# Attention feeding a SmeLU feed-forward on one core: four output tiles summed in two parts of d_ff, fillers joined, planner's times replaced

## The chip, the core and the metric

The kernel runs on one core of one Trainium2 chip. The metric is device time in microseconds (us), the median of three runs. A profile comes from one further execution, which has a time of its own; its span (first to last instruction) is a little shorter than that time. Engines are called as in the profile: PE (TensorE matmul), PEld (its weight loads), DVE (VectorE), ACT (ScalarE), POOL (GpSimd, which here only issues loads), SP (SyncE, which issues stores and some transposing DMAs).

## What is computed

```python
def sm_attn(qq, kk, vv):                      # softmax attention, scale 1/sqrt(64)
    ...
p_packed = sm_attn(p, k, v)                   # 32 packed rows per head attend to 576 tokens
out = sm_attn(q, p_packed, p_packed)          # 576 tokens attend to the 32 packed rows
x = out.transpose(0, 2, 1, 3).reshape(4608, 512)
h = x @ w_in                                  # (4608, 512) @ (512, 2048)
g = where(h >= 1, h, where(h <= -1, 0, (h + 1)**2 / 4))
return g @ w_out                              # (4608, 2048) @ (2048, 512)
```

q, k, v have 8 batches, 8 heads, 576 tokens and 64 channels; inputs and result are float32.

## The kernel before

**Stages of a batch.** For each of the 8 batches the kernel loads k, v and q (tokens folded 96 x 6), turns k and q (`trans`, on PE into PSUM and back by a copy to `kT`, `qT`; from batch 3 on by a transposing DMA that SP issues), forms the packed rows (`scores`: tile sp, exp by ACT into ex; `packed`: tile pk, then ppT and the reciprocal rs on DVE) and the weights of the second attention (`weights`: s, exp eT, column sums sm, ln, rc on ACT, then A on DVE, twice per batch). It never forms x: `mk` multiplies the packed rows by w_in (four tiles mp, cast to M), and `hidden_tile` (line 541) computes 128 rows of the hidden layer for the batch's 576 tokens as M times A. There are 16 hidden tiles per batch (index fi, along d_ff = 2048): four matmuls of 288 columns on PE (line 548), Prelu by ACT into x (line 553), an add-and-max on DVE or ACT (lines 558 and 560), and a min-and-multiply on DVE into hT (line 563).

**Output.** Two batches form a pair of 1152 tokens, nine output tiles of 128 tokens. `out_tile(pr, i)` (line 584) sums one of them: 16 steps, fi = 0 to 15, each one matmul of 128x512 (line 598, group "o"), hT as weights and the rows of w_out for that fi as moving data, into one PSUM buffer; then one copy of the sum to SBUF (`ob`, by ACT or DVE through the helper of line 319) and its stores from SP (line 604). Tiles 0 to 3 of a pair need the pair's first batch alone, tile 4 both. w_out comes in four loads of 512 rows, so fi 0 to 11 need the first three and fi 12 to 15 the last.

**Buffers.** PSUM has three buffers for everything else (`NW = 3`, pool psW) and two for output sums (`NO = 2`, pool psO). Prelu results have five (`NX`), `ob` six (`NB`).

**Order.** All instructions are handed out by `Plan`, when the kernel is built. Each piece of work is a task with an engine (or a choice of ACT and DVE, `both`), a cost in us from the table `C` (line 12), a key and its dependences. `run` (line 113) steps through an imagined time: of the tasks that are ready on an engine it takes the one with the lowest key that can start soon. Hidden tiles have the keys b to b + 1, output steps 100 and more, so an output step is taken where nothing else is ready. `land`, `load`, `half` and so on say when loads are thought to land, `slack` and `margin` how long after another engine's result PE is thought to be able to use it. Each engine then executes its list strictly in the order written; a wrong cost in the plan can put work that is ready behind work that isn't. The costs and times of the plan decide the order alone and no time on the chip.

**Fillers.** Until two output sums have been begun, where PE has nothing ready for more than a step, the plan writes matmuls of zeros of 256 columns (`idle`, line 661), each with its own weight load, which keep PE active.

**Loads.** POOL's queue issues, in this order: k, v, q of batch 0 in halves, w_in 0, w_in 1, w_out 0, w_in 2, w_out 1, w_in 3, w_out 2 (the third quarter), k of batch 1 in halves, v, q in halves, w_out 3 (the last quarter), the rest of p, and then k, q and v of later batches.

Of the kernel before, what the change touches and what calls it, by code (L numbers as in the profile page):

```python
# [8 lines left out]

C = dict(load=2.95, half=1.46, w_in=2.57, w_out=2.57, rest=1.25, out=9.0, p=4.05, land=1.75, xt=5.0, xland=11.0,
         tpp=0.06, tp=0.042, sc=0.034, pk=1.05, s2=0.25, sm=0.245, M=0.345, h=0.49, o=0.217, switch=0.05, join=0.15,
         pTc=0.1, Tca=1.12, Tcd=0.76, ex=0.82, ppT=0.42, ppo=0.41, ppa=0.4, ppd=0.2, rs=0.18, eT=0.74, ln=0.65, rc=0.68, A=0.82,
         Mca=1.0, Mcd=1.22, x=0.65, ta=0.683, td=0.457, hT=0.758, oba=0.585, obd=0.69,
         array=0.2, wake=1.2, warm=4.2, early=0.3, tell=0.04, feed=0.1, slack=0.6, margin=0.15, wait=0.5)
NW, NO, NX, NB = 3, 2, 5, 6
DW = 256
TURNED = 3


# [11 lines left out]
class Plan:  # L33
# [15 lines left out]
    def add(self, engines, cost, key, deps, fn, takes=None, readers=0, frees=None, mode=None, slack=None, after=0.0,  # L49
            holds=0.0):  # L50
        engines = (engines,) if isinstance(engines, str) else engines
        t = Task(engines, cost if isinstance(cost, dict) else {e: cost for e in engines}, key, deps, fn, takes, readers,
                 frees, mode, slack, after, holds)
        t.seq = len(self.tasks)
        self.tasks.append(t)
        return t

    def ready(self, t, e):
        at = 0.0
        for d in t.deps:  # L60
            if e == "PE":
                lag = 0.0 if d.on == "PE" else C["feed"] + (C["margin"] if t.slack is None else t.slack)
            else:
                lag = C["array"] if d.on == "PE" else C["tell"] if d.on != e else 0.0
            at = max(at, d.end + lag)
        if t.takes:
            rooms = self.rooms[t.takes]
            for j in range(len(t.readers)):
                room = rooms[(self.count[t.takes] + j) % len(rooms)]
                if room is None:  # L70
                    return None
                at = max(at, room + (C["feed"] if e == "PE" else 0.0))
        return at
# [39 lines left out]
    def run(self, idle):  # L113
        self.line = [t.seq for t in self.tasks if t.engines == ("DMA",)]
        left = {}
        given = {e: [] for e in self.ENGINES}
        for t in self.tasks:
            left[t] = len(t.deps)
            for d in t.deps:
                d.users.append(t)  # L120
            if not t.deps:
                for e in t.engines:
                    given[e].append(t)
        n = len(self.tasks)
        while n:
            best = None
            for e in self.ENGINES:
                c = self.choose(e, given, n)
                if c is not None and (best is None or c[0] < best[0]):
                    best = c[0], e, c[1]  # L130
            if self.count["O"] < 3:
                c, step = self.choose("PE", given, n), DW / 2400
                self.now["PE"] = max(self.now["PE"], C["wake"])
                if self.now["PE"] < C["warm"]:
                    step *= 2
                if (c is None or c[0] > self.now["PE"] + step + C["early"]) and best is not None and best[0] > self.now["PE"]:
                    idle()
                    self.now["PE"] += step
                    continue
            assert best is not None  # L140
            at, e, t = best
            t.on = e
            cost = t.cost[e]
            if e == "PE" and t.mode is not None and t.mode != self.mode:
                cost += C["switch"]
                self.mode = t.mode
            self.now[e] = at + cost
            t.end = at + cost + t.after + (C["land"] if e == "DMA" else 0.0)
            if e == "DMA":
                del self.line[0]  # L150
            self.log.append((at, at + cost, e, t))
            if t.takes:
                room = self.rooms[t.takes]
                t.slots = [(self.count[t.takes] + j) % len(room) for j in range(len(t.readers))]
                self.count[t.takes] += len(t.slots)
                for n_, j in zip(t.readers, t.slots):
                    room[j] = None if n_ else t.end + t.holds
            if t.frees is not None:
                f, j = t.frees
                f.gone[j] = max(f.gone[j], t.end)  # L160
                f.readers[j] -= 1
                if f.readers[j] == 0:
                    self.rooms[f.takes][f.slots[j]] = f.gone[j]
            if len(t.engines) > 1:
                t.fn(e)
            elif e in ("ACT", "DVE"):
                t.fn(e)
            else:
                t.fn()
            for x in t.engines:  # L170
                given[x].remove(t)
            for u in t.users:
                left[u] -= 1
                if left[u] == 0:
                    for x in u.engines:
                        given[x].append(u)
            n -= 1
# [3 lines left out]
def kernel(  # L181
# [10 lines left out]
    nc = tc.nc  # L192
    f32 = mybir.dt.float32
    bf16 = mybir.dt.bfloat16
    AF = mybir.ActivationFunctionType
    ALU = mybir.AluOpType
# [3 lines left out]
    d_model, d_ff = moe_w_in.shape  # L200
    n_tokens = out.shape[0]
    P = 128
# [13 lines left out]
    KF = d_ff // P  # L216
# [8 lines left out]
    att = ctx.enter_context(tc.tile_pool(name="att", bufs=2))  # L225
# [7 lines left out]
    plan = Plan({"W": NW, "O": NO, "x": NX, "ob": NB})  # L233
    PE, ACT, DVE, DMA, SP = "PE", "ACT", "DVE", "DMA", "SP"
    add = plan.add
# [10 lines left out]
    zeros = const.tile([P, FW], bf16)  # L246
# [3 lines left out]
    w_out_sb = const.tile([P, KF, d_model], bf16)  # L250
# [18 lines left out]
    hT = hid.tile([P, KF, 2 * S], bf16)  # L269
# [44 lines left out]
    def both(fns, cost_a, cost_d, key, deps, **kw):  # L314

        return add((DVE, ACT), {ACT: cost_a, DVE: cost_d}, key, deps, fns, **kw)

    def copy(out_, in_):
        return lambda eng: nc.vector.tensor_copy(out_, in_) if eng == DVE else nc.scalar.copy(out_, in_)  # L319
# [264 lines left out]
    def out_tile(pr, i):  # L584
        box, prev = {}, []
        bs = range(2 * pr + i * P // S, 2 * pr + ((i + 1) * P - 1) // S + 1)

        end = 2 * pr + 2 == B and i + 1 == NT
        w = d_model // 2

        def spare():
            box["o2"] = wide([P, w], f32, "o2")

        def step(fi):
            if fi == 0:
                box["o"] = psO.tile([P, d_model], f32, tag="o", name="o")
            for o, cs in [(box["o"][:, :w], slice(w)), (box["o2"], slice(w, d_model))] if end else [(box["o"], slice(d_model))]:
                nc.tensor.matmul(o, hT[:, fi, i * P:(i + 1) * P], w_out_sb[:, fi, cs], start=(fi == 0), stop=(fi == KF - 1))  # L598

        def done(eng):  # L600
            box["ob"] = ops.tile([P, d_model], f32, tag="ob", name="ob")
            copy(box["ob"], box["o"])(eng)
            for a, n, dst in out_rows(pr, i):
                nc.sync.dma_start(dst, box["ob"][a:a + n])

        def done_last(eng):

            for j, (eng, queue, o) in enumerate(((ACT, nc.scalar, box["o"][:, :w]), (DVE, nc.sync, box["o2"]))):
                ob = ops.tile([P, w], f32, tag="ob" + str(j), name="ob" + str(j), bufs=1)
                copy(ob, o)(eng)  # L610
                for a, n, dst in sorted(out_rows(pr, i), key=lambda x: -x[1]):
                    queue.dma_start(dst[:, j * w:(j + 1) * w], ob[a:a + n])
        if end:
            prev = [add(PE, 0.0, 100 + pr * NT + i, [K[B - 1, "h"][-1]], spare, takes="W", readers=1)]
        for fi in range(KF):
            t = add(PE, C["o"], 100 + pr * NT + i, [wrote[b, fi] for b in bs] + prev + [L["out", fi // 4]],
                    lambda fi=fi: step(fi), mode=0, takes="O" if fi == 0 else None, readers=1, slack=C["slack"])
            step_of[pr, i, fi] = t
            prev = [t]
            if fi == 0:  # L620
                owner = t
        both(done_last if end else done, C["oba"], C["obd"], b_key(pr, i), prev, frees=owner, takes="ob", holds=C["out"])

    def b_key(pr, i):
        return -0.5
# [32 lines left out]

    o = psO.tile([P, d_model], f32, tag="o", name="o")
    plan.count["O"] = 1  # L660
    plan.run(lambda: nc.tensor.matmul(o[:, :DW], zeros[:, :P], zeros[:, :DW], start=True, stop=True))  # L661


# [28 lines left out]
```

## Time and profile before

| What | Value |
|---|---|
| Three runs | 251.41, 252.23 and 252.58 us; median 252.23 us |
| The profiled execution | 250.97 us |
| Its span | 249.2 us |
| Outside the span (250.97 - 249.2) | 1.8 us |
| Granted TensorE clock | 1.0 of full speed in every slice |

Times inside the profile count from the span's start. Rows of the views by line give the engine, the operation, its output and inputs, the number of instructions, their busy time and the mean ns of one. A matmul's own duration contains the way through the array and overlaps the next one's, so what one matmul costs in a row of them is read from the length of the row. Idle time of an engine is listed by what ended it. A row of the timeline merges instructions of one kind that follow each other: start, length, what, how many, and in brackets the idle time before.

### The profile page before, as it was taken

What the parts mean: (1) busy time and instruction counts of PE and PEld (TensorE: products, weight loads), DVE (VectorE), ACT (ScalarE), POOL (GpSimd) and SP (SyncE); (2) the same over time, 40 slices, a digit from 0 to 9 for tenths busy, and PEclk for the clock granted to TensorE, in tenths of its full rate; (3) what the DMA queues carried; (4) which work ended last, traced back from release to release, by engine and by line L of the source; (5) the groups of instructions that cost most, each with busy time, mean ns of one, the idle gap of its engine ahead of it and who ended that gap; (6) DMA issues with size and microseconds to landing.
All of it is one profiled execution on the core that took longest, in us unless ns stands there. A gap on an engine that the chain in (4) does not pass through costs nothing.

```text
span 249.2 us, 5464 instructions
## 1 busy us (share of the span) xinstructions
PE 234.8 (94%) x2187; PEld 140.9 (57%) x2220; DVE 181.7 (73%) x308; ACT 182.5 (73%) x294; POOL 29.7 (12%) x44
## 2 busy tenths in 40 slices
PE   7887887999999999999999999999999999999993
PEld 5655465467546666556565656656556465544452
DVE  5456979788999899698979985998569878930000
ACT  3368888899888899798798984997859796841110
POOL 8632433012001301111101000000000000000000
PEclk9999999999999999999999999999999999999999
DMA  6999999999999999999999932312112112133223
GB/s 99 196 207 207 206 203 195 204 240 204 193 182 217 165 190 193 208 183 188 223 191 223 218 76 53 79 42 49 42 42 45 43 42 45 42 84 86 54 74 84
DMA packets 54825, 34.37 MB, mean 138 GB/s; under 512 B 27536, under 2 KB 50320, under 8 KB 54800
## 3 DMA queue, kind: packets, MB, share of 16 engines
q0 software_dynamic: 24672, 18.55, 49.9%
q1 hardware_dynamic: 29968, 15.34, 31.7%
q8 instruction: 17, 0.28, 0.4%
q10 hardware_dynamic: 160, 0.13, 0.2%
q14 instruction: 8, 0.07, 0.1%
HBM read 37.22 MB, written 9.44 MB: 187 GB/s over the span
## 4 chain that ended last, share of the span: by engine, by line
PE 76%; DMA 13%; ACT 3%; POOL 3%; issue 2%; DVE 2%; DVEq 0%; ACTq 0%; POOLq 0%
PE o L598 44%; PE h L548 22%; DMA w_in_sb<-in_moe_w_in_dram 7%; DMA q<-in_q_dram 6%; PE mp L493 3%; PE sp L397 2%; PE pk L417 1%; PE sm L461 1%; PE s L451 1%; PE tp L376 1%; DVE pT L319 1%; POOL w_in_sb L285 1%; ACT eT L456 1%; POOL k L259 1%; PE pk L423 1%
## 5 line engine op out<-in xcount | busy, mean ns | idle before, releaser
L598 PE MATMUL o<-w_out_sb,hT 128*128 128x512 bf16 (+1 forms) x559 | 135.6, 373 | 2.1 <-issue 1.1
L563 DVE SCALAR_TENSOR_TENSOR hT<-x 128x576 bf16<-128x576 f32 x128 | 93.2, 754 | 8.3 <-PE o L598 3.5
L598 PEld LDWEIGHTS <-hT 128*128 128x128 bf16 x592 | 56.1, 98 | 53.7 <-issue 4.8
L553 ACT ACTIVATE x<-h 128x576 f32<-128x576 f32 x128 | 77.2, 653 | 12.1 <-PE h L548 8.3
L548 PE MATMUL h<-A,M 128*128 128x288 bf16 x512 | 76.0, 286 | 1.4 <-ACT M L319 0.5
L548 PEld LDWEIGHTS <-M 128*128 128x128 bf16 x512 | 49.3, 98 | 24.1 <-ACT M L319 1.0
L558 DVE TENSOR_SCALAR x<-x 128x576 f32<-128x576 f32 x84 | 38.5, 459 | 11.8 <-ACT x L553 10.9
L319 ACT COPY ob<-o 128x512 f32<-128x512 f32 (+1 forms) x23 | 13.2, 576 | 32.1 <-PE o L598 32.1
L560 ACT ACTIVATE x<-x 128x576 f32<-128x576 f32 x44 | 29.4, 683 | 0.5
L319 DVE COPY ob<-o 128x512 f32<-128x512 f32 (+1 forms) x14 | 9.4, 669 | 25.8 <-PE o L598 25.7
L319 DVE CAST M<-mp 128x1024 bf16<-128x1024 f32 x16 | 19.4, 1218 | 2.8 <-PE mp L493 2.8
L319 ACT CAST M<-mp 128x1024 bf16<-128x1024 f32 x16 | 15.8, 1012 | 1.2 <-PE mp L493 1.2
L400 ACT ACTIVATE ex<-sp 96x768 bf16<-96x768 f32 x16 | 12.9, 806 | 3.2 <-PE sp L397 3.1
L472 DVE SCALAR_TENSOR_TENSOR A<-eT,rs,rc 128x576 bf16<-128x576 bf16 x16 | 13.0, 812 | 2.1 <-ACT rc L469 2.1
L259 POOL DMA_DIRECT2D k<-in_k_dram x10 | 7.5, 746 | 56.5 <-DMA kT<-k 40.0
L456 ACT ACTIVATE eT<-s,rs 128x576 bf16<-128x576 f32 x16 | 11.2, 736 | 2.8 <-PE s L451 2.6
L493 PE MATMUL mp<-w_in_sb,ppT 64*32 64x512 bf16 x256 | 10.7, 381 | 2.6 <-DMA w_in_sb<-in_moe_w_in_dram 2.2
L465 ACT ACTIVATE ln<-sm 128x576 f32<-128x576 f32 x16 | 10.4, 648 | 2.2 <-PE sm L461 2.1
L661 PE MATMUL o<-zeros 128*128 128x256 bf16 x68 | 10.6, 301 | 1.2 <-DVE zeros L247 1.2
L469 ACT ACTIVATE rc<-ln 128x576 f32<-128x576 f32 x16 | 10.9, 683 | 0.5
L259 POOL DMA_DIRECT2D q<-in_q_dram x10 | 7.6, 759 | 26.2 <-DMA qT<-q 12.7
L397 PEld LDWEIGHTS <-kT 128*128 128x128 bf16 x192 | 7.4, 98 | 2.6 <-DVE kT L319 0.6
(47 smaller groups left out, 114.4 us busy)
## 6 DMA issues: line engine op xcount, KB each, us to landing
out_dram<-ob SPq DMA_DIRECT2D x23, 192.0 KB, 2.5
v<-in_v_dram POOLq DMA_DIRECT2D x7, 576.0 KB, 18.4
k<-in_k_dram POOLq DMA_DIRECT2D x6, 576.0 KB, 12.4
q<-in_q_dram POOLq DMA_DIRECT2D x6, 576.0 KB, 14.0
out_dram<-ob SPq DMA_DIRECT2D x24, 128.0 KB, 2.8
w_in_sb<-in_moe_w_in_dram POOLq DMA_DIRECT2D x4, 512.0 KB, 14.7
w_out_sb<-in_moe_w_out_dram POOLq DMA_DIRECT2D x4, 512.0 KB, 16.8
out_dram<-ob SPq DMA_DIRECT2D x23, 64.0 KB, 2.0
```

Of the source, the lines that this page charges most:

```text
L259: nc.gpsimd.dma_start(tok[nm, b][:, hs].rearrange("p h c d -> p h (c d)"), SRC[nm][b, hs].rearrange("h (p c) d -> p h (c d)", c=NC))
L319: return lambda eng: nc.vector.tensor_copy(out_, in_) if eng == DVE else nc.scalar.copy(out_, in_)
L400: nc.scalar.activation(ex()[:, :, i].rearrange("p e x a n -> p e (x a n)"), box["sp"], AF.Exp, scale=scale)
L456: nc.scalar.activation(box["eT"], box["s2"][:, :, :HALF], AF.Exp, scale=rs()[:, g, 1:])
L472: nc.vector.scalar_tensor_tensor(A()[:, g], box["eT"], rs()[:, g, :1], box["rc"], ALU.mult, ALU.mult)
L493: nc.tensor.matmul(mp[a * NP:(a + 1) * NP, g], pp_of(y, h), w_in_sb[y * D:(y + 1) * D, h // 2, f * FW:(f + 1) * FW], start=True, stop=True)
L548: nc.tensor.matmul(h[:, hf, :HALF], T[b, "M"][:, g, fi * P:(fi + 1) * P], T[b, "A"][:, g, hf], start=(g == 0), stop=(g == G - 1))
L553: nc.scalar.activation(box["x"], box["h"][:, :, :HALF], AF.Prelu, bias=-1.0, alpha=0.5)
L558: nc.vector.tensor_scalar(x, x, 1.0, 0.0, ALU.add, ALU.max)
L560: nc.scalar.activation(x, x, AF.Relu, bias=1.0)
L563: nc.vector.scalar_tensor_tensor(hT[:, fi, col:col + S].rearrange("p (a t) -> p a t", a=2), box["x"], 1.0, box["x"], ALU.min, ALU.mult)
L598: nc.tensor.matmul(o, hT[:, fi, i * P:(i + 1) * P], w_out_sb[:, fi, cs], start=(fi == 0), stop=(fi == KF - 1))
```

## The change

Three things are done.

1. The output steps of tiles 0 to 3 of the first pair are cut at fi = 12. The first twelve steps are one PSUM sum; a new operation `kept` (by ACT or DVE) copies it to a new SBUF tile `part` (128x512 float32, four buffers) and so frees the PSUM buffer. The last four steps are a second sum in another PSUM buffer, and the final operation, on DVE alone, adds the PSUM sum and `part` into `ob`. All other output tiles are as before.
2. Fillers are gathered until the next real PE task and written as matmuls of up to 512 columns.
3. The plan's table `C` is replaced. Costs that differ: load 2.95 to 3.5666, land 1.75 to 2.0125, xt 5.0 to 6.5, pk 1.05 to 0.9765, s2 0.25 to 0.2862, M 0.345 to 0.2415, join 0.15 to 0.1604, td 0.457 to 0.489, obd 0.69 to 0.6276, tell 0.04 to 0.034, feed 0.1 to 0.085, slack 0.6 to 0.51, margin 0.15 to 0.1717.

```diff
+        cuts = [12, KF] if pr == 0 and i < 4 else [KF]
...
         def step(fi):
-            if fi == 0:
+            if fi == 0 or fi in cuts:
                 box["o"] = psO.tile([P, d_model], f32, tag="o", name="o")
...
-                nc.tensor.matmul(o, hT[:, fi, i * P:(i + 1) * P], w_out_sb[:, fi, cs], start=(fi == 0), stop=(fi == KF - 1))
+                nc.tensor.matmul(o, hT[:, fi, i * P:(i + 1) * P], w_out_sb[:, fi, cs], start=(fi == 0 or fi in cuts), stop=(fi + 1 in cuts))
+
+        def kept(eng):
+            box["part"] = att.tile([P, d_model], f32, tag="part", name="part", bufs=4)
+            copy(box["part"], box["o"])(eng)
 
         def done(eng):
             box["ob"] = ops.tile([P, d_model], f32, tag="ob", name="ob")
-            copy(box["ob"], box["o"])(eng)
+            if len(cuts) > 1:
+                nc.vector.tensor_tensor(box["ob"], box["o"], box["part"], ALU.add)
+            else:
+                copy(box["ob"], box["o"])(eng)
...
-                    lambda fi=fi: step(fi), mode=0, takes="O" if fi == 0 else None, readers=1, slack=C["slack"])
+                    lambda fi=fi: step(fi), mode=0, takes="O" if fi == 0 or fi in cuts else None, readers=1, slack=C["slack"])
...
-            if fi == 0:
+            if fi == 0 or fi in cuts:
                 owner = t
-        both(done_last if end else done, C["oba"], C["obd"], b_key(pr, i), prev, frees=owner, takes="ob", holds=C["out"])
+            if fi + 1 in cuts[:-1]:
+                first = both(kept, C["oba"], C["obd"], b_key(pr, i), prev, frees=owner)
+        if len(cuts) > 1:
+            add(DVE, C["obd"], b_key(pr, i), prev + [first], done, frees=owner, takes="ob", holds=C["out"])
+        else:
+            both(done_last if end else done, C["oba"], C["obd"], b_key(pr, i), prev, frees=owner, takes="ob", holds=C["out"])
...
-                    idle()
+                    fill += DW
                     self.now["PE"] += step
                     continue
...
+            while e == "PE" and fill:
+                w = min(fill, FILL)
+                idle(w)
+                fill -= w
...
-    plan.run(lambda: nc.tensor.matmul(o[:, :DW], zeros[:, :P], zeros[:, :DW], start=True, stop=True))
+    plan.run(lambda w: nc.tensor.matmul(o[:, :w], zeros[:, :P], zeros[:, :w], start=True, stop=True))
```

The first pair's nine tiles keep their 144 output matmuls, and all matmul shapes but the fillers' stay. Four copies (`kept`) are new, and four copies to `ob` become adds. The changed program's order, engine by engine, can be read from the built program; the prediction uses it.

More of the change, by code (lines that the diff above doesn't have):

```diff
@@ L8 @@
 from concourse._compat import with_exitstack
[L12 to L16, printed above, removed]
+C = dict(load=3.5666, half=1.46, w_in=2.57, w_out=2.57, rest=1.25, out=9, p=4.05, land=2.0125, xt=6.5, xland=11, tpp=0.06, tp=0.042, sc=0.034, pk=0.9765, s2=0.2862, sm=0.245, M=0.2415, h=0.49, o=0.217, switch=0.05, join=0.1604, pTc=0.1, Tca=1.12, Tcd=0.76, ex=0.82, ppT=0.42, ppo=0.41, ppa=0.4, ppd=0.2, rs=0.18, eT=0.74, ln=0.65, rc=0.68, A=0.82, Mca=1, Mcd=1.22, x=0.65, ta=0.683, td=0.489, hT=0.758, oba=0.585, obd=0.6276, array=0.2, wake=1.2, warm=4.2, early=0.3, tell=0.034, feed=0.085, slack=0.51, margin=0.1717, wait=0.5)
 NW, NO, NX, NB = 3, 2, 5, 6
-DW = 256
+DW, FILL = 256, 512
 TURNED = 3
@@ L123, in run @@
                     given[e].append(t)
-        n = len(self.tasks)
+        n, fill = len(self.tasks), 0
         while n:
```

## The prediction

> **What bounds the kernel now.** First the waits of PE, then the busy time by stretches.
>
> ```profile
> engine line waited for: us in total, times, longest us
> PE mp L493 <- DMA w_in_sb<-in_moe_w_in_dram: 2.2, 3, 1.0
> PE tp L376 <- DMA q<-in_q_dram: 1.6, 3, 0.6
> ...
> PE h L548 <- DVE pT L319: 0.3, 1, 0.3
> ```
> ```profile
> core 0: us, PE busy (x) PEld busy (x) DVE busy (x) ACT busy (x) POOL busy (x), PEclk, DMA share, GB/s
> 20.00:33.00 13.00, 11.26 (x85) 6.50 (x83) 10.93 (x19) 11.63 (x19) 3.94 (x6) 1.00 1.25 205
> 33.00:41.00 8.00, 6.86 (x122) 5.50 (x122) 6.42 (x13) 6.30 (x11) 2.68 (x4) 1.00 1.30 204
> 41.00:50.00 9.00, 7.87 (x100) 4.22 (x100) 7.42 (x9) 7.29 (x11) 1.53 (x2) 1.00 1.46 197
> 50.00:75.40 25.40, 24.63 (x276) 15.60 (x279) 22.99 (x39) 22.97 (x35) 2.32 (x3) 1.00 1.30 204
> 75.40:100.00 24.60, 24.39 (x231) 15.64 (x234) 23.26 (x39) 22.89 (x39) 3.43 (x4) 1.00 1.26 189
> 100.00:245.00 145.00, 143.39 (x1175) 82.11 (x1195) 100.19 (x166) 102.33 (x168) 3.92 (x5) 1.00 0.54 102
> ```
>
> PE waits for loads up to about 41 us and then hardly at all: 24.63 of 25.40, 143.39 of 145.00. So from 50 us the end is set by the PE work left over. Only early idle time can be won: 1.7 + 1.1 + 1.1 us in the three stretches to 50 us, and about 2 us more that is hidden because a lone matmul is booked as busy for its whole way through the array (0.38 us for an output step that costs 0.22 in a row). From 50 to 100 us DVE and ACT are nearly full too (90 to 95%).
>
> What one piece costs on PE is read where it runs in a row:
>
> ```profile
> 179.22 1.96 PE h L548 x16
> 181.18 3.88 PE o L598 x18
> ```
> ```profile
> 215.55 29.77 PE L598 MATMUL o<-w_out_sb,hT 128*128 128x512 bf16 x150
> ```
>
> Sixteen h matmuls take 1.96 us: a hidden tile (four) 0.49 us. Eighteen output steps take 3.88: 0.216 us each. The tail, 121 full and 32 half-width matmuls by the program's order (150 records), confirms it: 29.77 / 137 = 0.217.
>
> [...]
>
> **The change part by part.**
>
> ```profile
> 33.59 0.68 PE L376 MATMUL tp<-ident,k 96*128 96x96 bf16 x12 [0.51 <-DMA k<-in_k_dram]
> ...
> 37.53 1.24 PE L598 MATMUL o<-w_out_sb,hT 128*128 128x512 bf16 x5
> 38.61 0.86 PE L417 MATMUL pk<-ex,v 96*128 96x64 bf16 x24
> ...
> 40.86 0.68 PE L376 MATMUL tp<-ident,q 96*128 96x96 bf16 x12 [0.58 <-DMA q<-in_q_dram]
> ...
> 46.24 2.97 PE L598 MATMUL o<-w_out_sb,hT 128*128 128x512 bf16 x13
> 49.05 0.65 PE L548 MATMUL h<-A,M 128*128 128x288 bf16 x4
> ```
> ```profile
> 45.53 0.68 ACT L469 ACTIVATE rc<-ln 128x576 f32<-128x576 f32 x1
> ```
> ```profile
> 46.25 0.82 DVE L472 SCALAR_TENSOR_TENSOR A<-eT,rs,rc 128x576 bf16<-128x576 bf16 x1 [0.25 <-ACT rc L469]
> ```
>
> *More output steps early.* Before, two PSUM buffers hold tiles 0 and 1 up to fi 11, 24 steps, and no more can go until the last quarter of w_out lands. In the changed order 33 steps stand before pk (39 before the second tp of q) and 52 before batch 1's first hidden tile, where now 24 and 40 do. All other PE work up to that tile is the same, so 12 x 0.216 = 2.6 us less is left there.
>
> *When that tile starts.* Now at 49.05. PE first: up to the k turn at 33.59 the new order has 12 hidden matmuls more and one output step less (1.25 us), which fit in the idle time there, as M's third cast moves forward on ACT. From 33.59 to the end of tp q it has 16 output steps more and 12 h matmuls fewer: +2.0 us, against 0.6 us of idle time, so tp q comes about 1.2 us later (42.05). Then s, eT, sm, ln, rc and A follow with ACT's and DVE's durations, and rc ends near 47.6 instead of 46.2, A near 48.4 instead of 47.1. But now A waits 2 us for PE, which does 13 steps in front; in the new order only three stand there. First hidden tile at about **48.5 us**: 0.5 earlier. Lead 2.6 + 0.5 = **3.1 us**. I take 47.7 to 50 as its bounds (A straight behind today's end; 1.5 us of waits that I missed).
>
> *The copies.* Prices:
>
> ```profile
> L319 ACT COPY ob<-o 128x512 f32<-128x512 f32 x22 | 12.9, 585 | 29.3 <-PE o L598 29.3
> L319 DVE COPY ob<-o 128x512 f32<-128x512 f32 x13 | 8.9, 687 | 1.3 <-PE o L598 1.2
> L433 DVE TENSOR_TENSOR ppT<-pk,p 64x256 bf16<-64x256 f32 x7 | 2.8, 406 | 0.0
> L433 DVE TENSOR_TENSOR ppT<-pk,p 64x128 bf16<-64x128 f32 x2 | 0.6, 283 | 0.0
> ```
>
> Four `part` copies, three on DVE and one on ACT by the order: 3 x 0.687 + 0.585 = 2.6 us. The add at 128x512 isn't in the trace; its nearest kin read one PSUM and one SBUF operand, 283 and 406 ns for 128 and 256 elements, 0.96 ns an element: 406 + 256 x 0.96 = 0.65 us, about the copy that it replaces. Bounds 0.58 (ACT's copy) and 0.75 (the hT row below); I take 0.65, since the kin has the same operands. All four adds are on DVE; of the copies that they replace ACT does three now. Each add queues ahead of other DVE work: the first, behind tile 0's last four steps, stands ahead of both A of batch 1. Those steps need w_out's last quarter:
>
> ```profile
> 27.25 0.75 POOL L287 DMA_DIRECT2D w_out_sb<-in_moe_w_out_dram  x1 [1.28 <-DMA w_out_sb<-in_moe_w_out_dram]
> ```
> ```profile
> w_out_sb<-in_moe_w_out_dram POOLq DMA_DIRECT2D x4, 512.0 KB, 16.8
> ```
>
> It lands near 27.25 + 16.8 = 44. The steps are through at 45.8, the first rc of batch 1 not before 46.3, so the add hides; each us by which the load came later than 45 would delay A, M and PE by as much.
>
> *Fillers.* Joined pairs have the same columns; all stand before 20 us, where w_in's landing ends the waits (2.2 us above): 0, at most +-0.1.
>
> *Stores and loads.*
>
> ```profile
> 242.52 1.11 SPq L604 DMA_DIRECT2D out_dram<-ob  x2
> ```
>
> All eight stores of tiles 0 to 3 now stand ahead of batch 3's transposes on SP, at 0.55 us an issue, but the turned k isn't needed before batch 3's sp, after 70 us: 0. POOL's loads wait for turns and pk that come up to 1.2 us later while its queue has batch 2's loads still under way: 0, to 0.5 if a queue ran dry.
>
> *Batch 1's hidden stage, 48.5 to 75 us.* This takes part of the lead back.
>
> ```profile
> L563 DVE SCALAR_TENSOR_TENSOR hT<-x 128x576 bf16<-128x576 f32 x128 | 93.2, 754 | 8.3 <-PE o L598 3.5 <-ACT x L560 0.7 <-PE sp L397 0.5
> L553 ACT ACTIVATE x<-h 128x576 f32<-128x576 f32 x128 | 77.2, 653 | 12.1 <-PE h L548 8.3 <-DVE hT L563 3.4
> L558 DVE TENSOR_SCALAR x<-x 128x576 f32<-128x576 f32 x84 | 38.5, 459 | 11.8 <-ACT x L553 10.9
> L319 DVE CAST M<-mp 128x1024 bf16<-128x1024 f32 x16 | 19.4, 1218 | 2.8 <-PE mp L493 2.8
> L319 ACT CAST M<-mp 128x1024 bf16<-128x1024 f32 x16 | 15.8, 1012 | 1.2 <-PE mp L493 1.2
> ```
> ```profile
> 75.39 1.24 PE L548 MATMUL h<-A,M 128*128 128x288 bf16 x8
> ```
>
> Between batch 1's last A and batch 2's last A I summed both lists with start-to-start times (0.70 for hT, 0.56 for Prelu, 0.46 for the add-and-max; durations overlap by some 0.06 to 0.1 us): DVE 23.2 to 23.9 us, ACT 23.2 to 24.5, together 46.4 to 48.4. PE has fewer ready steps to bridge with: tiles 0 to 3 are nearly done, and tile 4 needs batch 1's hT. The order shows it: between the two sm and the 24 mp stand 3 steps, now 12 and sp. mp needs both ln to free PSUM, so PE idles there about 1 us. Walking ACT's queue (16 Prelu, two ex, four turns, then eT to rc, 24.5 us from 47.6) gives the last rc near 72.9 and A near 73.8, as now; then nine steps, and batch 2's first hidden tile at about 75.0, now 75.39. By then the order has 104 steps done against 95, less one sp of 12 (0.35 us): 9 x 0.216 - 0.35 = 1.6 us ahead, and 0.4 us earlier. Lead kept: **2.0 us**; 1.1 us is lost to waits.
>
> *Afterwards.* Batch 2's stage holds 25.6 us of PE work in the new order (61 output steps stand between its first and last part), DVE 22.6 and ACT 23.5. PE is the longer, as in all later stages. Lead stays 2.0 us, and the tail (tile halves, last stores) is as before.
>
> **Sum.** 250.97 - 2.0 = 249.0 us on the profiled execution's scale. That execution lies 1.26 us below the median of 252.23, so the forecast for a median is 252.23 - 2.0 = **250.2 us**.
>
> **Rivals.** One row more is needed, batch 3's first hidden tile:
>
> ```profile
> 95.92 2.34 PE L548 MATMUL h<-A,M 128*128 128x288 bf16 x16
> ```
>
> *The lead is kept whole.* If DVE and ACT hold 95% and the mp wait is filled, nothing is given back, and the present wait at 50.7 (h for pT, 0.3 to 0.5) goes too: 3.5 us, 248.7. For it: DVE and ACT reach 94% together from 75.4 to 100. Against: the few steps in front of mp.
>
> *DVE and ACT become the bound.* From batch 1's A (48.4) to batch 3's A they have, by the same sums, 47.9 + 46.5 = 94.4 us on two engines after the change, 85.5 before (two copies, three casts of M and three hidden tiles more inside the stretch). At a use u of both, A of batch 3 ends at 48.4 + 47.2/u. The new order has 6.8 us more PE work done at batch 3's first hidden tile, which now starts at 95.92. Lead = 6.8 + 95.9 - 48.4 - 47.2/u: 1.9 us at u = 0.90, 0 at 0.87, -1.2 at 0.85. So below 0.87 it is slower than before; at 0.84, with hidden tiles in the fixed order waiting for ACT's turns and casts, 252.23 + 1.9 = 254.1 us. For it: between the A of batches 1 and 2 these sums give 46.4 / (2 x 26.5) = 0.875 now. Against: PE was the one waited for there, and busy time gives 0.905 from 50 to 75.4 and 0.938 from 75.4 to 100.
>
> *Queueing eats it.* If batch 1's chain passes through the fuller PE, ACT and DVE queues 1.5 us later than I walked it (first hidden tile at 50), the lead at batch 2 is some 0.5 us: 251.7, no difference. That the cut does nothing, because the extra sums don't fit, is excluded by the order: 52 steps against 40.
>
> **How the numbers follow.** Forecast (gain 1.3 to 3 us) 0.48; lead whole 0.14; queueing, no difference 0.23; DVE and ACT the bound, slower 0.15. Within 0.5%, 1.26 us, a measurement of this kernel can't tell a change. Faster by over that 0.48 + 0.14 = 0.62, same 0.23, slower 0.15. The range takes in the whole lead with some 0.3 us of scatter (248.4) and u down to 0.87 (252.4); below and above lie about 0.2.
>
> **What would show it.** Right: 39 output steps before the second tp of q; batch 1's first hidden tile within 48 to 49.5 us; `part` copies and adds of 0.55 to 0.75 us; PE's waits around batch 2's sm and mp 1 us or more; DVE and ACT over 90% from 50 to 100 us; batch 2's first hidden tile near 75; no wait of PE after 100. Wrong: first hidden tile after 50, A of batch 1 queued behind the first add, waits of PE on hT or x between 75 and 100 us, or loads that land later than now.

## The result, and the profile after

Run in turns with the kernel before on one chip, the changed kernel took 250.05 us (median of 7 runs, 249.75 to 250.78), the kernel before 251.41 us (7 runs, 250.81 to 252.84). The ratio is 0.9933, its 95% interval 0.9906 to 0.9959: faster by 0.67%, about 1.7 us. The profiled execution took 249.87 us with a span of 247.8 us (before: 250.97 and 249.2).

The waits of PE in the changed kernel, then its busy time in the stretches that the prediction shows of before:

```profile
engine line waited for: us in total, times, longest us
PE mp L494 <- DMA w_in_sb<-in_moe_w_in_dram: 2.2, 3, 1.1
...
PE o L601 <- DVE hT L564: 0.6, 1, 0.6
PE h L549 <- ACT M L320: 0.5, 1, 0.5
```
```profile
core 0: us, PE busy (x) PEld busy (x) DVE busy (x) ACT busy (x) POOL busy (x), PEclk, DMA share, GB/s
20.00:33.00 13.00, 12.15 (x93) 7.36 (x92) 11.23 (x19) 11.75 (x19) 3.89 (x6) 1.00 1.26 206
33.00:41.00 8.00, 8.00 (x123) 5.58 (x122) 7.25 (x13) 6.49 (x10) 2.95 (x4) 1.00 1.31 206
41.00:50.00 9.00, 8.53 (x99) 4.00 (x97) 7.73 (x12) 6.63 (x10) 1.53 (x2) 1.00 1.46 195
50.00:75.40 25.40, 24.60 (x270) 14.95 (x269) 23.43 (x42) 23.87 (x36) 2.32 (x3) 1.00 1.28 209
75.40:100.00 24.60, 24.60 (x238) 14.59 (x237) 20.39 (x36) 22.41 (x36) 3.07 (x4) 1.00 1.27 209
100.00:245.00 145.00, 143.86 (x1199) 82.91 (x1197) 101.03 (x169) 106.63 (x173) 3.95 (x5) 1.00 0.54 98
```

The idle time of PE up to 50 us has shrunk from 1.74 + 1.14 + 1.13 = 4.0 us to 0.85 + 0 + 0.47 = 1.3 us: 2.7 us more work is done early. From 50 to 75.4 us PE is as busy as before (24.60, before 24.63), with 0.8 us of waits.

The timeline of PE in the changed kernel, from the second transposes of q to batch 3's first hidden tile:

```profile
42.25 0.68 PE L377 MATMUL tp<-ident,q 96*128 96x96 bf16 x12
...
49.06 0.65 PE L549 MATMUL h<-A,M 128*128 128x288 bf16 x4 [0.47 <-ACT M L320]
...
72.73 0.39 PE L601 MATMUL o<-w_out_sb,hT 128*128 128x512 bf16 x1 [0.56 <-DVE hT L564]
73.05 0.84 PE L494 MATMUL mp<-w_in_sb,ppT 64*32 64x512 bf16 x24
...
75.80 1.63 PE L549 MATMUL h<-A,M 128*128 128x288 bf16 x12
...
101.64 1.63 PE L549 MATMUL h<-A,M 128*128 128x288 bf16 x12
```

**The lead** tells where the time came from and where part of it went back. It is the PE work that stands before a batch's first hidden tile in one kernel and not in the other, less the time by which that tile starts later. Each piece is priced by what it costs in a row (0.216 us an output step and 0.123 an h, as in the prediction; a transpose tp 0.042, an sp 0.029).

- Batch 1: 12 steps, 2.6 us, and 49.06 against 49.05. Lead 2.6 us.
- Batch 2: 9 steps more and twelve sp (0.35 us) fewer, 1.6 us, and 75.80 against 75.39. Lead 1.2 us.
- Batch 3: 30 steps and 24 mp more and twelve sp fewer, 6.8 us, and 101.64 against 95.92, 5.7 later. Lead 1.1 us.
- The end: 249.2 - 247.8 = 1.4 us by the spans.

So 2.6 us are won before 49 us, 1.4 us are lost between 49 and 76 us, and nothing moves much after that.

### The profile page after: what moved, and what is told of

Read it like the earlier page. It is cut to its first block, busy times and chain, and to the rows that moved or that the text cites. A ratio compares the mean times of both kernels' runs of the same rounds, so it can differ in the third digit from the quotient of the medians.

```text
span 247.8 us, 5398 instructions
## 1 busy us (share of the span) xinstructions
PE 237.5 (96%) x2191; PEld 137.5 (55%) x2191; DVE 180.7 (73%) x312; ACT 186.2 (75%) x294; POOL 29.3 (12%) x44
## 4 chain that ended last, share of the span: by engine, by line
PE 79%; DMA 10%; DVE 6%; ACT 2%; issue 1%; POOL 1%; ACTq 0%; POOLq 0%
PE o L601 47%; PE h L549 21%; DMA w_in_sb<-in_moe_w_in_dram 8%; PE mp L494 3%; DVE hT L564 3%; DMA k<-in_k_dram 3%; PE pk L418 2%; PE sp L398 2%; PE tp L377 2%; PE sm L462 1%; DVE x L559 1%; PE s L452 1%; PE pk L424 1%; DVE pT L320 1%; ACT rc L470 1%
## 5 line engine op out<-in xcount | busy, mean ns | idle before, releaser
L601 PE MATMUL o<-w_out_sb,hT 128*128 128x512 bf16 (+1 forms) x592 | 144.5, 374 | 0.7 <-DVE hT L564 0.6
L564 DVE SCALAR_TENSOR_TENSOR hT<-x 128x576 bf16<-128x576 f32 x128 | 94.5, 755 | 5.4 <-ACT x L561 2.6
L549 PE MATMUL h<-A,M 128*128 128x288 bf16 x512 | 75.1, 286 | 0.5 <-ACT M L320 0.5
L559 DVE TENSOR_SCALAR x<-x 128x576 f32<-128x576 f32 x87 | 39.9, 458 | 11.0 <-ACT x L554 11.0
L561 ACT ACTIVATE x<-x 128x576 f32<-128x576 f32 x41 | 27.2, 683 | 0.1
L320 ACT COPY ob<-o 128x512 f32<-128x512 f32 (+1 forms) x19 | 10.9, 575 | 19.4 <-PE o L601 19.3
L320 ACT CAST M<-mp 128x1024 bf16<-128x1024 f32 x22 | 21.3, 1019 | 3.2 <-PE mp L494 3.2
L320 DVE CAST M<-mp 128x1024 bf16<-128x1024 f32 x10 | 12.1, 1220 | 6.4 <-PE mp L494 6.4
L260 POOL DMA_DIRECT2D q<-in_q_dram x10 | 7.4, 744 | 47.6 <-DMA qT<-q 33.3
L676 PE MATMUL o<-zeros 128*128 128x512 bf16 (+1 forms) x39 | 10.8, 406 | 1.2 <-DVE zeros L248 1.2
```

Of the source, the lines that this page charges most:

```text
L260: nc.gpsimd.dma_start(tok[nm, b][:, hs].rearrange("p h c d -> p h (c d)"), SRC[nm][b, hs].rearrange("h (p c) d -> p h (c d)", c=NC))
L549: nc.tensor.matmul(h[:, hf, :HALF], T[b, "M"][:, g, fi * P:(fi + 1) * P], T[b, "A"][:, g, hf], start=(g == 0), stop=(g == G - 1))
L559: nc.vector.tensor_scalar(x, x, 1.0, 0.0, ALU.add, ALU.max)
L561: nc.scalar.activation(x, x, AF.Relu, bias=1.0)
L564: nc.vector.scalar_tensor_tensor(hT[:, fi, col:col + S].rearrange("p (a t) -> p a t", a=2), box["x"], 1.0, box["x"], ALU.min, ALU.mult)
```

## The experiments

Two theories were set against each other. **The cut makes the gain**: the cut alone lets PE do more early, and the plan's new values matter little. **The gain needs both**: what counts is where the early steps stand, and the values of the plan decide that. Beside this stood the question of what takes 1.4 us back. In the table the steps are those before batch 1's first hidden tile, and the next column says when that tile starts; leads are in us against the kernel before (that at the end by the spans), and the ratio to the kernel before stands with its interval. No leads are given for the fillers alone, since no other piece of the order moves. Tiles and leads are of one execution each. Up to the first turn of batch 1's k the order of two tiles cut, of copies twice, of the add-and-max narrow and of turned by DMA is that of the changed kernel, yet that turn starts 0.44 us later in copies twice and 0.65 to 0.76 us later in the other three, behind later loads; their tiles and leads at batch 1 contain that.

| Kernel | Steps | Tile at | Lead batch 1 | Lead batch 2 | End | Ratio |
|---|---|---|---|---|---|---|
| before | 40 | 49.05 | | | | 1 |
| changed | 52 | 49.06 | 2.6 | 1.2 | 1.4 | 0.9933 (0.9906 to 0.9959) |
| cut alone | 52 | 52.90 | -0.3 | -2.6 | -2.6 | 1.0121 (1.008 to 1.0162) |
| times and fillers, no cut | 36 | 49.08 | -0.9 | -1.8 | -3.2 | 1.0121 (1.0084 to 1.0158) |
| fillers alone | 40 | | | | | 0.9987 (0.9958 to 1.0017) |
| two tiles cut | 55 | 49.83 | 2.5 | 0.9 | 0.7 | 0.9939 (0.991 to 0.9968) |
| old load and land | 64 | 55.58 | 0.2 | -2.3 | -2.4 | 1.0059 (1.0039 to 1.008) |
| old tell, feed, slack, margin | 52 | 49.77 | 2.4 | 0.1 | -0.2 | 0.9995 (0.9978 to 1.0012) |
| copies to part twice | 52 | 50.15 | 1.5 | -0.6 | -0.4 | 0.9992 (0.9973 to 1.0012) |
| copies to part narrow | 52 | 49.18 | 2.5 | 1.2 | 1.5 | 0.9927 (0.99 to 0.9954) |
| batch 1's add-and-max narrow | 52 | 49.73 | 1.9 | 1.1 | 1.3 | 0.9912 (0.989 to 0.9933) |
| turned by DMA from batch 2 on | 52 | 49.70 | 1.9 | -2.9 | -7.7 | 1.0252 (1.0216 to 1.0287) |

### The cut alone

Of the change only the cut: against the changed kernel, the old table `C` and fillers of 256 columns.

```diff
-DW, FILL = 256, 512
+DW, FILL = 256, 256
-C = dict(load=3.5666, ... margin=0.1717, wait=0.5)
+C = dict(load=2.95, ... margin=0.15, wait=0.5)
```

> The cut of the four tiles with the plan's old times and the old 256-column fillers. Theory (the cut makes the gain: more output steps go into PE's idle time before batch 1's first hidden tile, and part is given back while DVE and ACT work on batch 1): this order has 52 output steps before that tile, as the changed kernel, but 94 instead of 104 before batch 2's first, so some of the gain stays: a median about 250.6, 0.8 below the kernel before, first hidden tile of batch 1 at 49 to 50.5 us. Rival (the new times make the gain): no difference from the kernel before, about 251.4.

It took 254.45 us (before in the same turns 251.21), 1.2% slower than before, although 52 steps stand before batch 1's first hidden tile here too. PE's, ACT's and DVE's timelines of this kernel:

```profile
41.44 0.68 PE L381 MATMUL tp<-ident,q 96*128 96x96 bf16 x12
41.95 2.11 PE L605 MATMUL o<-w_out_sb,hT 128*128 128x512 bf16 x9
43.99 0.32 PE L456 MATMUL s<-qT,ppT 64*32 64x288 bf16 x8
...
49.18 0.68 PE L381 MATMUL tp<-ident,k 96*128 96x96 bf16 x12
...
50.35 0.67 PE L381 MATMUL tp<-ident,k 96*128 96x96 bf16 x12
...
52.90 0.65 PE L553 MATMUL h<-A,M 128*128 128x288 bf16 x4 [1.66 <-DVE kT L324]
```
```profile
43.30 0.40 ACT L324 COPY ppT<-ppT 64x256 bf16<-64x256 bf16 x1
```
```profile
52.09 1.42 DVE L324 COPY kT<-tp 128x1152 bf16<-128x1152 bf16 x2
```

Two things stand in the wrong place. The chain s, eT, sm, ln, rc, A, which everything waits for, starts 1.1 us later (s at 43.99, in the changed kernel at 42.85). Nine steps, 2.1 us, stand between the last transposes of q and the first s; but s needs the copy of ppT too, which in ACT's list stands behind other work and ends only at 43.70, so without the nine steps s could have come some 0.3 us earlier, not 2. And both transposes of batch 2's k stand before batch 1's first hidden tile; that tile needs one of the three PSUM buffers, and they are held (by these two and by tpp) until DVE copies kT out from 52.09 on, although batch 1's A has ended at 50.2. So the steps that were done early are paid for by a chain that starts late and a tile that waits for a buffer. The theory that the cut alone makes the gain fell here.

### The times and the fillers without the cut

```diff
-        cuts = [12, KF] if pr == 0 and i < 4 else [KF]
+        cuts = [KF]
```

> The new times and joined fillers without the cut. Theory (the cut makes the gain): 36 output steps stand before batch 1's first hidden tile, fewer than the 40 of the kernel before, so no gain: 251 to 252.3. Rival (the new times make the gain): as the changed kernel, about 250.0.

254.29 us, 1.2% slower than before. Batch 1's first hidden tile starts when it does in both other kernels (49.08), but only 36 steps stand ahead of it. PE of this kernel waits where the changed kernel has steps:

```profile
39.22 0.51 PE L418 MATMUL pk<-ex,v 96*128 96x64 bf16 x12 [0.68 <-ACT ex L401]
...
40.98 0.84 PE L494 MATMUL mp<-w_in_sb,ppT 64*32 64x512 bf16 x8 [0.45 <-DVE ppT L434]
...
44.50 0.40 PE L462 MATMUL sm<-eT,onesblk 128*128 128x288 bf16 x2 [0.59 <-ACT M L320]
```

With four steps fewer done, this kernel lies 0.9 us behind at batch 1. By batch 2 it is 1.8 us behind (PE waits 1.16 us for ACT's x at 51.41) and at the end 3.2; what takes the last 1.4 us was not traced.

The two halves are each a loss of 1.2%, which neither expectation of either run foresaw, and together a gain of 0.7%: they must not be added.

### Fillers alone

The kernel before with fillers gathered to 512 columns (the diff is against before).

```diff
-                    idle()
+                    fill += DW
```

> The kernel before with the fillers joined to 512 columns, nothing else. Theory (same columns, all before 21 us, where loads set the pace): no difference, 251.0 to 251.5. Rival (half as many weight loads free PE early): 250.7 or less.

251.41 us against 251.65: no difference. Of the three parts of the change this one does nothing that can be measured.

### Two tiles cut

```diff
-        cuts = [12, KF] if pr == 0 and i < 4 else [KF]
+        cuts = [12, KF] if pr == 0 and i < 2 else [KF]
```

> The changed kernel with tiles 0 and 1 alone cut: two copies fewer, the four adds become two; 55 output steps before batch 1's first hidden tile instead of 52, 104 before batch 2's first as before. Theory (the gain is steps placed early less what DVE and ACT give back): the same or up to 0.7 us faster than the changed kernel, 249.3 to 250.0. Rival (the gain goes with the number of tiles cut): half of it, about 250.7.

250.09 us, ratio 0.9939, no difference from the changed kernel that can be measured. With tiles 0 and 1 cut the plan puts 55 steps before batch 1's first hidden tile, three more than with four tiles cut. The gain of the change can be had with two copies and two adds; the number of cut tiles is not what sets it.

### More steps early

The changed kernel with the old `load` and `land`; the other new values stay.

```diff
-load=3.5666, land=2.0125
+load=2.95, land=1.75
```

> The changed kernel with the old load and land times, all other times new: the plan takes loads for earlier than they are and writes 64 output steps, not 52, ahead of batch 1's first hidden tile, most of them ahead of s of batch 1. Theory, amended after the first runs (early steps pay only where PE would idle; in front of batch 1's chain from q to A they delay it, and all that follows): s of batch 1 two or more us later than in the changed kernel, first hidden tile at 51.5 us or later, median 251.5 to 254. Rival (what counts is how many steps are done early): 12 more steps are 2.6 us, median about 247.5.

253.11 us, slower than before by 0.6%. There are 64 steps early, 24 more than before, but PE's timeline shows where:

```profile
43.40 1.46 PE L601 MATMUL o<-w_out_sb,hT 128*128 128x512 bf16 x6
45.34 0.51 PE L332 MATMUL tpp<-ident,p_nat 128*128 128x128 bf16 x6 [0.49 <-DMA p_nat<-in_p_dram]
...
46.24 1.69 PE L601 MATMUL o<-w_out_sb,hT 128*128 128x512 bf16 x7
47.86 0.32 PE L452 MATMUL s<-qT,ppT 64*32 64x288 bf16 x8
...
55.58 0.65 PE L549 MATMUL h<-A,M 128*128 128x288 bf16 x4 [0.57 <-DVE kT L320]
```

The second s comes at 47.86 (changed: 44.08), behind thirteen steps and behind the transposes tpp, which the plan with these values puts ahead of their load. Batch 1's first hidden tile starts 6.5 us later, behind three turns more and with a wait for DVE's kT, which eats the 6.7 us of more work (the steps and those turns). More early steps are not better: the same lesson as the cut alone, with the cut tiles, the fillers and most values as in the changed kernel.

### The old safety times

The changed kernel with the old values of the four times that say how long after another engine's result PE can use it.

```diff
-tell=0.034, feed=0.085, slack=0.51, margin=0.1717
+tell=0.04, feed=0.1, slack=0.6, margin=0.15
```

> The changed kernel, but of the plan's new values four go back: tell, feed, slack and margin, the times that say how long after another engine's result TensorE can use it. Its order has 52 output steps before batch 1's first hidden tile as the changed kernel has, and 93 before batch 2's (104 in the changed kernel). Theory (what decides is how many steps stand where TensorE would idle without standing ahead of batch 1's chain; the load and cost values give that, and these four only shift a few steps): batch 1's first hidden tile at 48.8 to 49.8 us, ratio to the kernel before 0.990 to 0.997. Rival (the four values are what places batch 1's and batch 2's chains right; without them output steps or turns stand ahead of the chain again, as with the old plan): batch 1's or batch 2's first hidden tile over 1 us later than in the changed kernel, ratio 1.002 to 1.012.

251.27 us against 251.31, so all of the gain is gone; the ratio lies between the two expectations. The first theory's number for batch 1 holds (49.77 us, lead 2.4), but its ratio doesn't, and the rival's delay of over 1 us is not there. Here the gain is lost in batch 1's stage. PE of this kernel:

```profile
72.26 0.61 PE L601 MATMUL o<-w_out_sb,hT 128*128 128x512 bf16 x2 [0.88 <-DVE hT L564]
...
74.02 0.39 PE L601 MATMUL o<-w_out_sb,hT 128*128 128x512 bf16 x1 [0.39 <-DVE hT L564]
74.48 0.67 PE L549 MATMUL h<-A,M 128*128 128x288 bf16 x4
```

Batch 2's first hidden tile starts 1.3 us earlier than in the changed kernel, but with 11 steps fewer in front of it (93, changed 104), and PE waits 0.88 and 0.39 us on hT. The lead there is 0.1. Values that differ by 0.1 us or less decide over the whole gain.

### The copies to part made twice

```diff
             copy(box["part"], box["o"])(eng)
+            copy(box["part"], box["o"])(eng)
```

> The changed kernel with each copy to part done twice: six DVE copies and two on ACT instead of three and one, 2.6 us more work on the two engines, the same order on PE. Theory (DVE and ACT take part of the lead back in batch 1's stretch): batch 1's second A and its first hidden tile come 0.5 to 1.5 us later, and the median is 0.4 to 1.2 us above the changed kernel's, 250.5 to 251.3. Rival (the copies lie beside other work and cost nothing): 250.0, first hidden tile at 49.1 as in the changed kernel.

251.26 us, the gain is gone (ratio 0.9992); 2.6 us more of copies cost 1.5 us by the ratios (0.9992 against 0.9933) and 1.8 by the spans (249.6 against 247.8). PE of this kernel, with the instruction order of the changed kernel:

```profile
38.24 0.81 PE L601 MATMUL o<-w_out_sb,hT 128*128 128x512 bf16 x3 [0.51 <-DVE part L320]
...
50.15 0.65 PE L549 MATMUL h<-A,M 128*128 128x288 bf16 x4 [0.47 <-ACT M L320]
...
53.87 0.33 PE L377 MATMUL tp<-ident,k 96*128 96x96 bf16 x4 [0.77 <-DVE pT L320]
```

The first hidden tile comes 1.1 us later than in the changed kernel. Of this 0.44 is not the copies': the turn of k is that late (34.20, changed 33.76), before any copy to `part` and behind a longer wait for w_in (1.25 us at 30.16, changed 0.60 at 29.70). Then PE waits 0.51 us for a PSUM buffer that the doubled copy holds. 0.7 us more are lost between this tile and batch 2's, beginning with the wait for pT, whose copies stand behind a doubled one on DVE. Without the late load the spans give 1.4 us, close to the 1.5 of the ratios.

### The copies to part made narrow

Each copy to `part` takes 64 of 512 columns, and the adds are plain copies. This leaves the first twelve steps out of the result of tiles 0 to 3.

```diff
-            copy(box["part"], box["o"])(eng)
+            copy(box["part"][:, :64], box["o"][:, :64])(eng)
-                nc.vector.tensor_tensor(box["ob"], box["o"], box["part"], ALU.add)
+                nc.vector.tensor_copy(box["ob"], box["o"])
```

> The changed kernel, same order, but part takes 64 of 512 columns and the adds are copies of the second sum alone; left out is the first twelve steps' contribution to tiles 0 to 3. Theory (the four copies on DVE and ACT cost about 0.6 us of time for each us, as doubling them showed): 0.8 to 1.3 us faster than the changed kernel, 248.8 to 249.3. Rival (the first copy lies in idle time and only the second was dear): 250.0.

249.86 us, ratio 0.9927: no gain over the changed kernel that can be measured, and batch 2's first hidden tile at 75.81 (changed 75.80). The copies as they are cost nothing that can be measured; made twice they cost. So they lie in slack, and what slack is left behind them doesn't hold a second set.

### Batch 1's add-and-max made narrow

The changed kernel's order, but DVE's add-and-max of batch 1 takes 64 of 576 columns (the rest of that operation is left out for batch 1).

```diff
-                nc.vector.tensor_scalar(x, x, 1.0, 0.0, ALU.add, ALU.max)
+                xs = x[:, :, :32] if b == 1 else x
+                nc.vector.tensor_scalar(xs, xs, 1.0, 0.0, ALU.add, ALU.max)
```

> The changed kernel with the same order, but VectorE's add-and-max on batch 1's hidden tiles works on 64 of 576 columns (leaves out the rest of that step for batch 1, so half of that batch's activation is not computed). This frees VectorE of about 0.35 us per tile, some 4 us in all, between 52 and 75 us. Theory (the part of the lead that is lost before batch 2 is lost on VectorE, which from 61 to 72.7 us works back to back and on which the output step at 72.73 waits): batch 2's first hidden tile starts 0.7 to 1.4 us earlier than in the changed kernel (near 74.4 to 75.1 instead of 75.80), and the time is 0.7 to 1.4 us below the changed kernel's, ratio to the kernel before about 0.988 to 0.9905. Rival (ScalarE's list of Prelus, casts, turns and then eT, ln, rc sets batch 2's first hidden tile, VectorE only happens to be full): that tile starts within 0.3 us of 75.80, and the ratio stays at 0.992 to 0.995.

249.43 us, ratio 0.9912, between the two expectations. The groups by line and PE's timeline of this kernel:

```profile
L560 DVE TENSOR_SCALAR x<-x 128x64 f32<-128x64 f32 x12 | 2.3, 189 | 0.9 <-ACT x L554 0.8
```
```profile
69.56 0.59 PE L602 MATMUL o<-w_out_sb,hT 128*128 128x512 bf16 x2 [0.16 <-DVE hT L565]
...
71.47 0.41 PE L462 MATMUL sm<-eT,onesblk 128*128 128x288 bf16 x2 [0.21 <-ACT eT L457]
...
73.41 0.41 PE L494 MATMUL mp<-w_in_sb,ppT 64*32 64x512 bf16 x8 [0.33 <-ACT ln L466]
...
75.91 1.63 PE L549 MATMUL h<-A,M 128*128 128x288 bf16 x12
```

Twelve operations of 0.46 us became 0.19, 3.2 us of DVE. In this execution loads landed late (k is turned at 34.43, changed 33.76) and batch 1's first hidden tile stands at 49.73, so the stage itself is compared: from there to batch 2's it takes 26.18 us, in the changed kernel 75.80 - 49.06 = 26.74. That is 0.56 us back of the 1.4 lost. Batch 1's last hT ends 1.45 us earlier by the same measure, and the wait of 0.56 for hT has gone, but in its place PE waits for ACT's eT and ln, 0.21 and 0.33. The ratios give 0.5 us too, though their intervals overlap. So DVE holds this stage by some 0.5 us, and right behind it ACT does.

### Turned by DMA from batch 2 on

Batch 2's k and q are turned by SP's transposing DMA, as from batch 3 on, which takes 48 transposes off PE and their copies off DVE and ACT.

```diff
-TURNED = 3
+TURNED = 2
```

> The changed kernel with batch 2's k and q turned by the transposing DMA as batch 3's are: 48 transposes leave PE (2.0 us) and four copies leave ACT (4.2 us), all in the stretch of batch 1's hidden tiles. Theory (DVE and ACT take the lead back there): 2 to 3.5 us faster than the changed kernel, 246.5 to 248.0. Rival (the transfers between 48 and 70 us are full, turned k and q land too late and batch 2's first hidden tile moves back): 250 or more, with waits of PE on turned k or q.

258.1 us, 2.5% slower. PE of this kernel:

```profile
77.56 4.92 PE L601 MATMUL o<-w_out_sb,hT 128*128 128x512 bf16 x22
82.41 0.44 PE L452 MATMUL s<-qT,ppT 64*32 64x288 bf16 x16
...
86.54 0.64 PE L549 MATMUL h<-A,M 128*128 128x288 bf16 x2 [1.70 <-DVE A L473]
```
```profile
88.00:90.00 2.00, 2.00 (x9) 1.21 (x9) 0.68 (x2) 1.08 (x2) 0.00 (x0) 0.50 1.23 176
```

With this the plan places batch 2's attention late: s at 82.41 (changed: 68.07), behind 22 steps in a row, and batch 2's first hidden tile at 86.54. It therefore says nothing on whether the turns' copies take the lead back. Order in another place explains only part of the loss: the lead is -2.9 us at batch 2's first hidden tile, but -7.7 at the end. Behind that tile PE's granted clock, the third number from the end in the row by stretch, is 0.50 from 88 to 92 us (0.59 in the two before, 0.80 from 92 to 95), which alone costs some 3 us, as an estimate from PE's busy time in these stretches. The six runs have mean clocks of 0.986 to 0.991. The rest was not traced.

## Why the prediction was right, and where it was not

**The twelve steps, 2.6 us: right.** 52 steps stand there, PE's idle time to 50 us fell by 2.7 us, and the second tp of q came at 42.25 (forecast 42.05).

**"First hidden tile at about 48.5 us: 0.5 earlier": wrong.** It starts at 49.06, as before. ACT's and DVE's timelines of the changed kernel:

```profile
44.46 0.74 ACT L457 ACTIVATE eT<-s,rs 128x576 bf16<-128x576 f32 x1 [0.47 <-PE s L452]
...
47.42 0.68 ACT L470 ACTIVATE rc<-ln 128x576 f32<-128x576 f32 x1
48.01 1.91 ACT L320 CAST M<-mp 128x1024 bf16<-128x1024 f32 x2
```
```profile
48.14 0.82 DVE L473 SCALAR_TENSOR_TENSOR A<-eT,rs,rc 128x576 bf16<-128x576 bf16 x1 [0.52 <-ACT rc L470]
48.88 0.68 DVE L320 COPY part<-o 128x512 f32<-128x512 f32 x1
```

The second eT waits 0.47 us for s, which stands behind two mp and two steps; rc ends at 48.1 (forecast 47.6) and A at 48.96 (48.4). Then the first cast of M, which ACT makes only after rc, ends about as late as A (48.01 and 1.0 us), and PE waits 0.47 us for it. The chain of batch 1 was walked without the steps inside it and without the cast behind it. The bounds, 47.7 to 50, held it.

**Batch 1's stage, "1.1 us is lost to waits": right in kind, 1.4 us in size.** DVE is busy for 92% and ACT for 94% of 50 to 75.4 us, as forecast. The wait sits on hT (0.56, at 72.73) and not on ln at mp; taking DVE's load away brings 0.56 us back. Both errors add: the lead at batch 2 is 1.2 us where 2.0 was forecast (tile at 75.80 instead of 75.0).

**"Lead stays 2.0 us": it does stay** (1.2, 1.1, then 1.4 at the end). From 75.4 to 100 us PE is the one that is full (24.60 of 24.60), DVE only 83%, so "over 90% to 100 us" was too high, and the rival in which DVE and ACT become the bound stayed out. That PE would not wait after 100 us came true: its last matmul ends at 243.86, and from 100 us to there it is busy all the time, where before 1.6 of 145 us were idle; this is where the lead goes from 1.1 to 1.4 us.

**The copies and adds at 0.65 us each, hidden: right.** The groups by line:

```profile
L610 DVE TENSOR_TENSOR ob<-o,part 128x512 f32<-128x512 f32 x4 | 2.8, 688 | 0.3 <-PE o L601 0.2
L320 DVE COPY part<-o 128x512 f32<-128x512 f32 x3 | 2.1, 689 | 0.2 <-PE o L601 0.2
```

The add, with one operand in PSUM and one in SBUF, measures 0.688 us, inside its bounds of 0.58 to 0.75; the copy to `part` of the same size takes 0.689 us on DVE. The narrow copies showed that they cost nothing as they are, the doubled ones that no second set would be hidden.

**Fillers at 0: right,** by their own experiment.

**The time.** 250.2 us was forecast and 250.05 measured. Part of that closeness is luck: the forecast took 2.0 us from a median of 252.23, the turns beside the changed kernel gave 251.41 for before, and the gain was 1.4 us by the medians and 1.7 by the ratio. Some tenths of a us of this may be no lead at all but the clock, which the working left out (see the last section). What the working had right is that it counted the steps in the finished order. Had it argued from the cut alone, as "12 more steps early, 2.6 us", it would have forecast the same for the cut alone, which is 3.2 us slower than before.

**Which values of the table matter** was narrowed, not settled. Without `load` and `land` the kernel is 0.6% slower than before, without the four safety times it equals before; the six costs (`pk`, `s2`, `M`, `join`, `td`, `obd`) and `xt` weren't tried by themselves, and of the 1.4 us in batch 1's stage only 0.56 are put to an engine by a run; the other 0.8 are not.

## What to carry to other kernels

Where a bound engine idles early, moving independent work there paid in these runs only where it stood behind, not ahead of, the chain that the next stage starts with: count the pieces between the chain's links in the finished order of each engine that the chain passes, since the same 52 early steps gained 0.7% in one order and lost 1.2% in another. When an enabling change and a table of scheduling costs are changed together, measure each alone before crediting either. And follow a lead from stage to stage: of the 2.6 us won here by batch 1's first hidden tile 1.4 were given back in the next stretch, in which DVE is busy for 92% and ACT for 94%.

## What the runs showed of the hardware

**PE fell to half its clock after an idle time of 1.95 us.** In the profiled execution of the cut alone a load of q came late. PE's timeline and its granted clock by stretches (the third number from the end of a row):

```profile
15.18 1.14 PE L381 MATMUL tp<-ident,q 96*128 96x96 bf16 x12 [1.95 <-DMA q<-in_q_dram]
```
```profile
15.00:15.50 0.50, 0.32 (x5) 0.32 (x6) 0.00 (x0) 0.00 (x0) 0.08 (x1) 0.62 1.23 201
15.50:18.00 2.50, 2.50 (x35) 2.19 (x33) 1.26 (x4) 0.85 (x2) 1.07 (x2) 0.50 1.24 206
18.00:18.50 0.50, 0.50 (x3) 0.14 (x1) 0.50 (x2) 0.00 (x0) 0.20 (x1) 0.50 1.25 207
18.50:19.00 0.50, 0.50 (x17) 0.14 (x16) 0.36 (x1) 0.06 (x1) 0.00 (x0) 0.97 1.24 207
```

Twelve transposes took 1.14 us instead of 0.68. The half clock lasts 0.38 + 2.5 + 0.5 + 0.03 = 3.4 us by these rows. Later in the same execution a wait of 1.66 us (at 52.90) left the clock at 1.00. With batch 2 turned by DMA it fell as well, behind 83.07 to 86.54 us, where PE is busy for 0.8 of 3.5 us, and stayed low for 6.8 us by the same working. Why the clock fell at these places and not at the wait of 1.66 us, no run shows. In the cut alone only 0.46 us of the delay was left by the next transposes of k (34.05 us, before 33.59), and its runs with a mean clock of 1.0 took 253.65 and 255.8 us, so the clock isn't what made that kernel slow.

**The kernel before loses clock more often than the changed order.** A stretch of 3.4 us at half clock lowers the mean clock of 249 us by 0.007, to 0.993. Beside the experiments, on three chips, the kernel before ran 62 times: 39 runs with a mean clock of 0.996 or more, median 251.2 us, and 23 with 0.993 or less, median 252.3. The changed order (the changed kernel, the copies made twice or narrow, the add-and-max narrow) ran 32 times, never below 0.996. So part of the measured gain may come from this, some 0.4 us as an estimate (23 of 62 times 1.1 us). No trace shows where the kernel before loses its clock or why the changed order keeps it, so this stays open.

**The same four copies cost nothing that can be measured when made once, and some 1.5 us when made twice**, though each took 0.59 (ACT) or 0.69 us (DVE): what an instruction costs here is what it exceeds the slack of its place by.
